# Fused sliding-window attention and MoE on one core: first loads in float32, batch 1 transposed on chip, chunk 0's second matmul in halves

## The chip, the cores and the metric

One core of one Trainium2 chip runs the whole program. The metric is the device time of one execution in microseconds (us), the median of a few runs. In these kernels TensorE does the matmuls, VectorE and ScalarE the elementwise work (in the kernel before 2352, 430 and 288 instructions), GpSimd issues the loads that cast float32 to bfloat16, and SyncE issues the stores and the DMA transposes.

The kernel before varies a good deal from run to run and from chip to chip: 343.7 to 351.1 us within a single set of runs. Times in us are therefore compared only within one set, on one chip; across sets the ratio to the kernel before is compared, which was run beside every set. Runs more than 1.5% above the fastest of their kernel are called slow and left out; this took away 5 of the 11 runs of the kernel before in the second set, 2 of 11 in the third and none in the first, although runs of 350 us occur in all three. So a difference between sets of less than about 0.01 shows little.

## The reference

```python
# q, k, v: float32 [batch 8, heads 8, seq 576, head_dim 64]
# scores = q k^T / 8 + ALiBi bias, causal window of 128, softmax, times v
scores = scale * np.matmul(q, k.transpose(0, 1, 3, 2))
mask = (rel >= 0) & (rel < 128)
scores = np.where(mask, scores + bias[None], -1e9)
attn = np.exp(scores - scores.max(-1, keepdims=True))
attn_out = np.matmul(attn / (attn.sum(-1, keepdims=True) + 1e-9), v)

# tokens of all batches in a row: 4608 x 512, then two matmuls with a gate
x = attn_out.transpose(0, 2, 1, 3).reshape(8 * 576, 512)
h = x @ w_in            # 512 x 2048
g = h * np.cos(h)
out = g @ w_out         # 2048 x 512, float32
```

## The kernel before

The operations are written in program order with their tile dependences; a list scheduler in the kernel assigns each a start with cost constants (`occ`, `lat`), and that fixes, before anything runs, the order of every engine's instructions. Each engine's program holds its list in that order, and in the traces an instruction whose data is late holds those behind it: in the kernel before, TensorE did nothing for the 9.9 us ahead of batch 1's scores, and GpSimd issued no load for 27.7 us while one waited.

Attention of a batch has nine units: eight of two heads and 256 tokens (`G` is 0 or 1), and a tail of 64 tokens. The MoE runs in nine chunks of 512 tokens: `moe1` (64 matmuls of 128x512 outputs and the gate) and `moe2` (64 more). Chunk c is interleaved with the attention of batch c+1. Chunk 2 is tokens 1024 to 1535 and batch 2 begins at token 1152, so chunk 2 needs the first outputs of batch 2's attention soon after they are made.

The loads and the places of q and k:

```python
        def load_piece(w, src, g):
            op("pool", [lambda e: e.dma_start(
                nat[w][0][:, 2 * g:2 * g + 2, :].rearrange("p a (h c) -> p (a h) c", h=4),
                src[0, :, 256 * g:256 * g + 256, :].rearrange("h (s j) d -> s h (j d)", j=2))],
               w=[("nat", w, 0, g)], dma=f"ld{w}0{g}", occ=720, lat=1500)

        def load_nat(w, src, b, t):
            rows = 128 if t < 4 else 64
            op("pool", [lambda e: e.dma_start(
                nat[w][b % 2][0:rows, t, :].rearrange("p (h d) -> p h d", h=H),
                src[b, :, 128 * t:128 * t + rows, :].rearrange("h p d -> p h d"))],
               w=[("nat", w, b % 2, t)] + ([("nat", w, 0, t // 2)] if b % 2 == 0 and t < 4 else []),
               dma=f"ld{w}{b % 2}n{t}", occ=900, lat=7 * rows)
```

For batches 1 to 7 q and k are transposed by DMA, block by block (ten DMA transposes a batch); batch 0 is transposed on TensorE:

```python
        def cross_transposes(b, blocks=range(NBLK)):
            i = b % 2
            for t in blocks:
                rows = 128 if t < 4 else 64
                for w in "qk":
                    op("sp", [lambda e, t=t, rows=rows, w=w: e.dma_start_transpose(
                        tr[w][i][:, :, 128 * t:128 * t + rows], nat[w][i][0:rows, t, :])],
                       r=[("nat", w, i, t)], w=[("tr", w, i, t, hf) for hf in range(2)],
                       dma=f"x{w}{i}{t}", occ=1000, lat=700 if t < 4 else 400, pri=3)
```

The attention output is transposed back either by DMA or on TensorE:

```python
        def x_back(b, u, s, i):
            if u[0] == "t":
                t0 = S * b + 512
                op("sp", [lambda e: e.dma_start_transpose(xT[:, :, t0:t0 + 64], xtl[i][:, :])],
                   r=[("xtl", i)], w=[k_ for pr in range(NPAIR) for k_ in xkeys(pr, t0, 64)],
                   dma=f"xt{i}", occ=700, lat=400, pri=2)
                return
            pr, G = u
            t0 = S * b + 256 * G
            if b >= 4 or (b > 0 and G == 0):
                op("sp", [lambda e: e.dma_start_transpose(
                    xT[:, pr, t0:t0 + 256].rearrange("p (r t) -> p r t", r=2), xnat[i][:, :])],
                   r=[("xnat", i)], w=xkeys(pr, t0, 256), dma=f"xb{i}", occ=700, lat=500, pri=2)
                return
            bank = SLOT[s][0]
            dst = ps[:, bank, :].bitcast(BF16)[:, 768:1024]

            def f(e):
                ins = None
                for r in range(2):
                    ins = e.transpose(dst[:, 128 * r:128 * r + 128],
                                      xnat[i][:, 128 * r:128 * r + 128], ident[:, :])
                return ins
            op("pe", f, r=[("xnat", i), "ident"], w=[("B", bank)], occ=120, lat=290, pri=0)
            flex(xT[:, pr, t0:t0 + 256], dst, [("B", bank)] + xkeys(pr, t0, 256), 256, 0)
```

The second matmul of a chunk, and the order of everything:

```python
        def moe2(c):
            gi = c % 2
            for t in range(4):
                tg = 4 * c + t
                bank = OB[tg % 2]
                oi = tg % NOB
                for fc in range(NFC):
                    op("pe", lambda e, t=t, fc=fc, bank=bank: e.matmul(
                        ps[:, bank, :], gT[gi][:, fc, 128 * t:128 * t + 128], w_out[:, fc, :],
                        start=(fc == 0), stop=(fc == NFC - 1)),
                       r=[("g", gi, fc, t // 2), ("wo", fc // 4)], w=[("B", bank)], occ=216, lat=379,
                       pri=6)
                row = CH * c + 128 * t
                halves = 2 if tg == 4 * NCH - 1 else 1
                wd = 512 // halves
                for hf in range(halves):
                    cs = slice(wd * hf, wd * hf + wd)
                    flex(ob[oi][:, cs], ps[:, bank, cs], [("B", bank), ("ob", oi, hf)], wd, 6)
            # ... [store of the tile]
```

```python
        load_piece("q", q, 0)
        load_piece("k", k, 0)
        constants()
        fills()
        load_v(0, (0, 1))
        masks()
        load_piece("q", q, 1)
        load_piece("k", k, 1)
        load_w_in(0)
        load_nat("q", q, 0, 4)
        load_nat("k", k, 0, 4)
        load_v(0, (2, 3, 4))
        for i, w in enumerate("qk"):
            first_transposes(w, 0, (4, 6)[i])
        for u in range(1, 4):
            load_w_in(u)
        load_w_out(0)
        load_w_out(1)
        for t in range(NBLK):
            load_nat("q", q, 1, t)
            load_nat("k", k, 1, t)
        load_w_out(2)
        load_w_out(3)
        load_v(1)
        us0 = units(0)

        def run(b, us, ns, n0):
            two = [(u, (n0 + j) % ns) for j, u in enumerate(us)]
            scores(b, two)
            for u, s in two:
                exps(b, u, s)
            for u, s in two:
                mask(b, u)
                pv(b, u, s)
                i = norm(b, u, s)
                x_back(b, u, s, i)
        run(0, us0[0:2], 4, 0)
        run(0, us0[2:4], 4, 2)
        for i, w in enumerate("qk"):
            first_transposes(w, 1, (3, 5)[i])
        first_tail(7)
        run(0, us0[4:6], 4, 0)
        run(0, us0[6:8], 4, 2)
        run(0, us0[8:9], 4, 0)
        order = [4, 5, 6, 7, 0, 1, 2, 3]
        for c in range(NCH):
            if c == 0:
                for i in range(NFC):
                    moe1_half(c, i // 8, i % 8, order[i % 8])
            else:
                for fc in range(NFC):
                    moe1(c, fc, 2 + fc % 6)
            if c + 1 < B:
                cross_transposes(c + 1)
                attention(c + 1)
            if c + 2 < B:
                for t in range(NBLK):
                    load_nat("q", q, c + 2, t)
                    load_nat("k", k, c + 2, t)
                load_v(c + 2)
            moe2(c)
```

The softmax here doesn't subtract the row's maximum and nothing guards it: scores larger than these inputs give would overflow.

## Time and profile before

| | before |
|---|---|
| median time | 344.8 us (3 runs, 344.6 to 346.2) |
| span of the profiled execution | 343.6 us |
| TensorE busy | 307.8 us |
| TensorE idle in 36 to 62 us | 9.9 us, mean granted clock 0.80 |
| TensorE idle in 105 to 120 us | 7.3 us, mean granted clock 0.66 |

Four lines of the page of the kernel before: the busy time of each engine; the busy tenths of TensorE and its granted clock in 40 slices of 8.6 us; and the shares of the chain of waits by engine.

```profile
PE 307.8 (90%) x2352; PEld 155.8 (45%) x2352; DVE 191.5 (56%) x430; ACT 203.7 (59%) x288; POOL 105.0 (31%) x133
...
PE   2689809989992899999998999899999999999996
...
PEclk9969967999997699999999999999999999999999
...
PE 77%; DMA 14%; POOL 5%; DVE 1%; ACT 1%; SPq 1%; issue 1%; POOLq 0%; DVEq 0%; ACTq 0%
```

The two dips in the TensorE row, at slices 6 and 13, are the two stalls; the clock row is below 9 beside them. The rest of the row is nearly full, so the kernel can only gain in those places, at the start, or by doing less on TensorE.

Four stretches of the kernel before, with busy time and number of instructions for each engine, then the granted clock, the DMA share and GB/s.

```profile
core 0: us, PE busy (x) PEld busy (x) DVE busy (x) ACT busy (x) POOL busy (x), PEclk, DMA share, GB/s
36.00:62.00 26.00, 16.14 (x120) 9.09 (x118) 7.54 (x19) 8.29 (x12) 0.00 (x0) 0.80 1.83 147
95.00:105.00 10.00, 9.45 (x101) 4.55 (x99) 4.59 (x13) 6.08 (x9) 0.00 (x0) 1.00 1.75 156
105.00:120.00 15.00, 7.68 (x53) 3.99 (x54) 4.04 (x10) 3.04 (x5) 3.64 (x5) 0.66 1.43 131
250.00:282.00 32.00, 31.95 (x260) 15.34 (x257) 22.61 (x51) 22.12 (x30) 0.00 (x0) 1.00 0.19 53
```

The last line is a batch in the steady part: 31.95 of 32.0 us busy. The lines of 36 and 105 us are the stalls.

TensorE's timeline of the kernel before, the instructions with a long idle time ahead of them (start, duration, instruction; in brackets the idle time and what ended it). The count at the end of a line depends on where the listing was cut.

```profile
51.32 1.15 PE L463 MATMUL ps<-qt,kt 64*128 64x256 bf16 x12 [9.87 <-DMA kt<-knat]
...
110.44 0.61 PE L674 MATMUL ps<-xT,w_inb 128*128 128x512 bf16 x1 [5.95 <-DMA xT<-xnat]
112.11 0.61 PE L674 MATMUL ps<-xT,w_inb 128*128 128x512 bf16 x1 [1.06 <-DMA xT<-xnat]
```

The first is batch 1's scores waiting for keys transposed by DMA. The other two are `moe1` of chunk 2 waiting for outputs of batch 2.

SyncE's queue of the kernel before: start and time taken by each issue.

```profile
44.21 3.21 SPq L425 DMA_TRANSPOSE kt<-knat  x1
...
99.50 1.26 SPq L425 DMA_TRANSPOSE qt<-qnat  x1
100.80 1.28 SPq L425 DMA_TRANSPOSE kt<-knat  x1
...
102.75 4.38 SPq L618 DMA_TRANSPOSE xT<-xnat  x3
```

Batch 3's transposes `qt` and `kt` (to 102 us) stand in the list ahead of batch 2's outputs `xT`, and each issue there takes about 1.3 us, for 128x256 (the last line is three of them, 4.38 us together) as for 128x512 elements. From issue to landing the transposes of k took 2.4 to 12.9 us in this run. GpSimd's queue of the kernel before:

```profile
34.05 0.89 POOL L310 DMA_DIRECT2D knat<-in_k_dram  x1
62.62 0.88 POOL L310 DMA_DIRECT2D qnat<-in_q_dram  x1 [27.67 <-DMA knat<-in_k_dram]
```

After the first load of k for batch 2 it waits 27.7 us. In the kernel the key `("nat", w, 0, t // 2)` makes block 1 of an even batch depend on block 0's landing.

The chain of waits of the kernel before in order of time (start, length, piece), as marks of progress: the block of `moe1` of chunk 1, the start of `moe2` of chunk 1, and `moe1` of chunk 2 with 53 matmuls left.

```profile
73.86 13.12 PE ps L674 x60
86.98 1.73 PE ps L704 x8
...
119.77 11.61 PE ps L674 x53
```

### The profile page before, as it was taken

To read this page: it belongs to the slowest core of one execution; us is meant where nothing else is said; L and a number is where in the kernel's file an instruction comes from. 1 tells how busy PE (TensorE), PEld (TensorE's weight loads), DVE (VectorE), ACT (ScalarE), POOL (GpSimd) and SP (SyncE) were. 2 spreads that over 40 slices of the span, in tenths; PEclk is the share of its full clock that TensorE was granted. 3 is DMA by queue.
4 is the path that set the end of the run, shared out by engine and by line. 5 is a ranking of instruction groups with operands and counts; after the bars stand their busy time and mean duration, and the time that the engine had idled before them with its cause. 6 is when DMAs were issued, how large, how long until landed. Compare 5 with 4: busy or idle time off the path is not lost.

```text
span 343.6 us, 6134 instructions
## 1 busy us (share of the span) xinstructions
PE 307.8 (90%) x2352; PEld 155.8 (45%) x2352; DVE 191.5 (56%) x430; ACT 203.7 (59%) x288; POOL 105.0 (31%) x133
## 2 busy tenths in 40 slices
PE   2689809989992899999998999899999999999996
PEld 1468604544450444454454444445544454444442
DVE  3558602568651385658656855784686768365000
ACT  5859703578543287459648865785688378465121
POOL 8997000379900489142434801300000000000000
PEclk9969967999997699999999999999999999999999
DMA  9999999999999999999997999972310220000212
GB/s 80 165 199 188 164 143 125 179 142 146 154 156 158 110 163 165 178 167 154 106 136 116 155 158 121 111 124 55 92 25 31 84 66 15 0 33 32 90 63 93
DMA packets 167405, 39.87 MB, mean 116 GB/s; under 512 B 158544, under 2 KB 162896, under 8 KB 167376
## 3 DMA queue, kind: packets, MB, share of 16 engines
q0 software_dynamic: 112576, 18.36, 80.2%
q1 hardware_dynamic: 54800, 21.12, 33.4%
q8 instruction: 19, 0.31, 0.4%
q14 instruction: 10, 0.08, 0.1%
HBM read 36.70 MB, written 9.44 MB: 134 GB/s over the span
## 4 chain that ended last, share of the span: by engine, by line
PE 77%; DMA 14%; POOL 5%; DVE 1%; ACT 1%; SPq 1%; issue 1%; POOLq 0%; DVEq 0%; ACTq 0%
PE ps L704 35%; PE ps L674 31%; DMA knat<-in_k_dram 5%; DMA xT<-xnat 5%; PE ps L463 4%; DMA kt<-knat 4%; PE ps L556 3%; PE ps L559 1%; POOL vp L319 1%; ACT p L499 1%; POOL w_inb L326 1%; SPq L425 1%; PE ps L542 1%; POOL qnat L303 1%; DVE p L517 1%
## 5 line engine op out<-in xcount | busy, mean ns | idle before, releaser
L704 PE MATMUL ps<-w_outb,gT 128*128 128x512 bf16 x576 | 140.9, 385 | 0.0
L674 PE MATMUL ps<-xT,w_inb 128*128 128x512 bf16 x512 | 116.8, 381 | 10.7 <-DMA xT<-xnat 10.1
L666 DVE TENSOR_TENSOR gT<-ps,cos 128x512 bf16<-128x512 f32 x144 | 94.3, 686 | 27.9 <-ACT cos L660 18.1
L660 ACT ACTIVATE cos<-ps,halfpi 128x512 f32<-128x512 f32 x144 | 94.2, 688 | 22.0 <-PE ps L674 14.0
L674 PEld LDWEIGHTS ps<-xT,w_inb 128*128 128x128 bf16 x512 | 48.5, 98 | 69.1 <-DMA xT<-xnat 12.2
L704 PEld LDWEIGHTS ps<-w_outb,gT 128*128 128x128 bf16 x576 | 52.6, 99 | 55.8 <-issue 3.7
L499 ACT ACTIVATE p<-ps 128x768 bf16<-128x768 f32 (+1 forms) x64 | 54.3, 917 | 34.9 <-PE ps L463 23.8
L310 POOL DMA_DIRECT2D qnat<-in_q_dram x36 | 32.6, 906 | 65.6 <-DMA qnat<-in_q_dram 35.9
L296 ACT ACTIVATE ob<-ps 128x512 f32<-128x512 f32 (+1 forms) x26 | 15.1, 581 | 55.5 <-PE ps L704 55.5
L319 POOL DMA_DIRECT2D vp<-in_v_dram x40 | 34.2, 918 | 44.1 <-PE ps L559 37.2
L310 POOL DMA_DIRECT2D knat<-in_k_dram x36 | 32.8, 912 | 4.9 <-DMA knat<-in_k_dram 4.8
L517 DVE TENSOR_TENSOR p<-p,emask 128x1024 bf16<-128x1024 bf16 x32 | 21.8, 686 | 16.2 <-ACT p L499 16.0
L598 DVE TENSOR_TENSOR xnat<-ps,rec 128x256 bf16<-128x256 f32 x64 | 26.9, 422 | 2.0
L463 PE MATMUL ps<-qt,kt 64*128 64x128 bf16 (+1 forms) x320 | 18.4, 255 | 10.7 <-DMA kt<-knat 9.9
L556 PEld LDWEIGHTS ps<-vp,p 128*128 128x128 bf16 x256 | 18.2, 102 | 18.4 <-issue 13.6
L522 DVE TENSOR_TENSOR p<-p,emask 128x256 bf16<-128x256 bf16 x32 | 9.0, 282 | 30.5 <-ACT p L499 30.1
L556 PE MATMUL ps<-vp,p 128*128 128x65 bf16 x256 | 23.2, 200 | 1.2 <-DVE p L517 0.9
L463 PEld LDWEIGHTS ps<-qt,kt 64*128 64x128 bf16 x320 | 12.9, 99 | 21.0 <-issue 19.0
L559 PE MATMUL ps<-vp,p 128*128 128x65 bf16 x192 | 21.3, 200 | 0.0
L596 DVE RECIPROCAL rec<-ps 128x4 f32<-128x4 f32 x64 | 11.2, 177 | 17.7 <-PE ps L559 17.4
L296 ACT ACTIVATE xT<-ps 128x256 bf16<-128x256 bf16 x15 | 5.7, 384 | 20.7 <-PE ps L628 20.3
L297 DVE COPY ob<-ps 128x512 f32<-128x512 f32 x11 | 7.6, 692 | 18.5 <-PE ps L704 18.5
(52 smaller groups left out, 167.0 us busy)
## 6 DMA issues: line engine op xcount, KB each, us to landing
out_dram<-ob SPq DMA_DIRECT2D x35, 256.0 KB, 2.6
vp<-in_v_dram POOLq DMA_DIRECT2D x32, 128.0 KB, 6.3
qnat<-in_q_dram POOLq DMA_DIRECT2D x28, 128.0 KB, 8.2
knat<-in_k_dram POOLq DMA_DIRECT2D x28, 128.0 KB, 9.1
w_inb<-in_moe_w_in_dram POOLq DMA_DIRECT2D x4, 512.0 KB, 10.4
w_outb<-in_moe_w_out_dram POOLq DMA_DIRECT2D x4, 512.0 KB, 19.7
xT<-xnat SPq DMA_TRANSPOSE x44, 3.2
qt<-qnat SPq DMA_TRANSPOSE x35, 6.5
```

The costliest lines, as they stand in the source:

```text
L310: op("pool", [lambda e: e.dma_start(nat[w][b % 2][0:rows, t, :].rearrange("p (h d) -> p h d", h=H), src[b, :, 128 * t:128 * t + rows, :].r ...
L319: op("pool", [lambda e, t=t, rows=rows: e.dma_start(vp[b % 2][0:rows, t, :, 0:64], v[b, :, 128 * t:128 * t + rows, :].rearrange("h p d -> ...
L463: ins = e.matmul(ps[:, banks[x], c0:c1], keys_ap(i, x, pr, kc), query_ap(i, x, pr, qb, 128 * nb), start=True, stop=True)
L499: op("act", lambda e: e.activation(P[i][:, :, lo:512], src_[:, :, lo:512], ACTF.Exp, scale=0.125), w=held + [("P", i)], occ=920 if u[1] el ...
L517: op("dve", lambda e: e.tensor_tensor(p, p, m, ALU.mult), r=[("P", i), ("EM", 2 * pr), ("EM", 2 * pr + 1)], w=[("P", i)], occ=605, lat=lat ...
L556: ins = e.matmul(o, P[i][:, x, d0:d0 + 128], V[:, kc, h, 0:65], start=True, stop=not two)
L559: ins = e.matmul(o, P[i][:, x, p0:p0 + 128], V[:, kc - 1, h, 0:65], start=False, stop=True)
L598: op("dve", lambda e: e.tensor_tensor(o, U[:, :, :, 0:64], rv[:, :, :, None].broadcast_to([128, 2, 2, 64]), ALU.mult), r=[("rec", ri)], w= ...
L660: op("act", lambda e: e.activation(cosb[ci][:, :], h, ACTF.Sin, bias=halfpi[:, 0:1]), r=["halfpi"], w=[("B", bank), ("cos", ci)], occ=586, ...
L666: op("dve", lambda e: e.tensor_tensor(o, h, cs, ALU.mult), r=[("cos", ci)], w=[("B", bank)] + keys, occ=606, lat=692, pri=3)
L674: op("pe", lambda e, kc=kc: e.matmul(ps[:, bank, :], w_in[:, kc, 128 * fc:128 * fc + 128], xT[:, kc, CH * c:CH * c + CH], start=(kc == 0), ...
L704: op("pe", lambda e, t=t, fc=fc, bank=bank: e.matmul(ps[:, bank, :], gT[gi][:, fc, 128 * t:128 * t + 128], w_out[:, fc, :], start=(fc == 0 ...
```

## The change

The change loads the first 256 tokens of q and k in float32 from SyncE's queue and casts them on VectorE or ScalarE; loads batch 1 in the pair layout (rows of 256 bytes in the buffer in place of 128) and transposes it on TensorE; does `moe2` of chunk 0 in two halves, so that the first half needs only half of `w_out`; loads v of batch 1 before the rest of `w_out`; transposes two blocks at once by DMA for batches 2 to 7; drops the shared keys; and gives the scheduler other costs for SyncE's queue. The name given to the change also says that sums of P times V are kept in score banks; that was so already, only the order of the banks is new.

```diff
-        free = {e: 0 for e in ENG}
+        free = {"pe": 1000, "act": 800, "dve": 1000, "pool": 1300, "sp": 1000}
...
-        tr = {w: [sb(f"{w}t{i}", [128, NPAIR, 640]) for i in range(2)] for w in "qk"}
+        tr = {w: [sb(f"{w}t{i}", [128, NBLK, NPAIR, 128]) for i in range(2)] for w in "qk"}
...
+        def load_first(w, src, hf, i):
+            op("sp", [lambda e: e.dma_start(
+                ob[i][:, :].rearrange("p (h c) -> p h c", h=4),
+                src[0, 4 * hf:4 * hf + 4, 0:256, :].rearrange("h (s j) d -> s h (j d)", j=2))],
+               ...)
+            o, x = nat[w][0][:, hf, :], ob[i][:, :]
+            op(("act", "dve"), {... activation Copy, or tensor_copy ...})
...
-               w=[("nat", w, b % 2, t)] + ([("nat", w, 0, t // 2)] if b % 2 == 0 and t < 4 else []),
+               w=[("nat", w, b % 2, t)],
...
-        def cross_transposes(b, blocks=range(NBLK)):
+        def cross_transposes(b):
             i = b % 2
-            for t in blocks:
-                rows = 128 if t < 4 else 64
+            for t0, t1 in ((0, 2), (2, 4), (4, 5)):
                 for w in "qk":
...
-                       dma=f"x{w}{i}{t}", occ=1000, lat=700 if t < 4 else 400, pri=3)
+                       dma=f"x{w}{i}{t0}", occ=1250, lat=1200 if t0 < 4 else 500, pri=3)
...
-                   dma=f"xt{i}", occ=700, lat=400, pri=2)
+                   dma=f"xt{i}", occ=1250, lat=400, pri=2)
...
         def moe2(c):
+            if c == 0:
+                for u in range(2):
+                    for t in range(4):
+                        moe2_mm(c, t, range(8 * u, 8 * u + 8), t)
+                    if u == 0:
+                        yield
+                for t in range(4):
+                    store(c, t, t)
+                return
...
-        for t in range(NBLK):
-            load_nat("q", q, 1, t)
-            load_nat("k", k, 1, t)
+        for g in range(2):
+            load_piece("q", q, 1, g)
+            load_piece("k", k, 1, g)
+        load_nat("q", q, 1, 4)
+        load_nat("k", k, 1, 4)
+        load_v(1)
         load_w_out(2)
         load_w_out(3)
-        load_v(1)
...
             if c + 1 < B:
-                cross_transposes(c + 1)
-                attention(c + 1)
+                us = units(c + 1)
+                if c == 0:
+                    for g in range(2):
+                        first_transposes("q", 1, g, (4 + 2 * g, 4 + 2 * g))
+                        first_transposes("k", 1, g, (5 + 2 * g, 5 + 2 * g))
+                    for g in range(0, 8, 2):
+                        run(1, us[g:g + 2], (2, 3))
+                    first_tail(1, 6)
+                    run(1, us[8:9], (2,))
+                else:
+                    cross_transposes(c + 1)
+                    for g in range(0, 9, 3):
+                        run(c + 1, us[g:g + 3], (1, 2, 3))
```

## The prediction

> **What bounds it now.** The page: span 343.6 us, TensorE busy 307.8; the chain of waits is 77% TensorE, 14% DMA. From 120 us on it is TensorE-bound: in 250 to 282 us, one batch, TensorE is busy 31.95 of 32.0 us. The loss lies early. TensorE's timeline: idle to 5.75 us, then about 5 us of gaps by 21 us, granted clock 0.50 in 20 to 25 us; 41.4 to 51.3 us, idle 9.9 us for batch 1's key transposes by DMA, then half clock to 55 us, some 2.2 us more; 105 to 120 us, idle 7.5 us for batch 2's transposed outputs, then half clock, some 2.8 us. [...] Later gaps add 2.5 us.
>
> **Why those gaps.** Each DMA transpose takes SyncE's queue 1.25 us to issue[...] (DMA queue's timeline); a batch has ten for q and k. From 82 to 107 us that queue issues without pause: batch 3's transposes stand ahead of batch 2's outputs. GpSimd's queue waits 27.7 us before batch 2's second load, as two blocks share one dependence key.
>
> **What the change does.**
> - First 256 tokens: four float32 loads on SyncE's queue, cast on chip in 0.3 to 0.6 us each. First scores at about 8 instead of 9.0 us; second pieces issue 2 us sooner. Gain 1.5 to 2.5 us.
> - Batch 1's q and k are loaded with rows twice as long and transposed on TensorE: adds 64 transposes, 3.4 us at 53 ns, and evictions of 0.6 to 0.7 us that hide on ScalarE and VectorE. Removes the 9.9 us wait and its cold stretch.
> - moe2 of chunk 0 in halves: 32 matmuls (6.9 us at 216 ns) need only half of w_out and fill the wait for batch 1. But v of batch 1 and the rest of w_out land at an estimated 45 to 50 us, so 3 to 4 us of waits remain. Net gain of this stage 6 to 8 us: chunk 1's moe1 starts near 64 instead of 73.9 us, the start included.
> - Six transposes per batch instead of ten: SyncE saves 5 us a batch. The false dependence is gone, so loads run ahead. The 105 to 120 us stall (10 to 11 us with the cold clock) falls to 1 to 4 us; gain about 8 us.
> - MoE arithmetic is unchanged. PV sums already share the score banks: nothing from that. Later batches stay at 32 us.
>
> Sum: 2 + 7 + 8 + 1.5 (later gaps), 18.5 to 20 us, nearly all on the chain, since TensorE was idle there.
>
> **Predicted: 325 us, 8 in 10 within 316 to 336.** Faster by over 2%: 0.90; within 2%: 0.08; slower: 0.02.
>
> **Right if:** no DMA-transpose wait of batch 1 in the chain; TensorE idle in 36 to 62 us under 5 us; chunk 1's moe1 starts at 60 to 67 us; idle in the stage of batch 2's outputs under 4 us; issue still 1.25 us for two-block transposes; span from chunk 1's start unchanged but for the lost stall.
>
> **Wrong if:** two-block transposes issue in twice the time (the stall near 100 us stays); loads run so deep in GpSimd's queue that v of batch 1, w_out or batch 2's output transposes land late; SyncE, in order, sits behind batch 3's late loads; the schedule, computed ahead with optimistic loads, puts TensorE on data not yet landed; the float32 loads contend with v, so the start gains nothing.

The 5 us a batch in the second stage takes the issue time as the same for two blocks, which was an estimate. The sum is 2 + 7 + 8 + 1.5 = 18.5 us. Some measured times beside those it uses: in the kernel before, the issues of k's transposes took 1.2 to 3.2 us, 1.28 in the median; batch 0's transposes on TensorE took 51 to 80 ns each (8 in 0.41 to 0.64 us), so 53 ns is an estimate; a copy of 128x512 out of a bank took 0.60 us on ScalarE and 0.69 on VectorE; 60 matmuls of 128x512 in a row took 13.12 us, 216 ns apart. Between 82 and 107 us SyncE's queue had one pause of 1.2 us, at 88 us. In the changed kernel a cast of 128x512 took 0.43 us on VectorE and 0.63 us on ScalarE.

## The result and the profile after

The changed kernel took 328.55 us (median of 4, 327.5 to 328.8) against 345.5 us for the kernel before beside it (4 runs). The ratio is 0.9511, interval 0.9472 to 0.9551. A ratio here is the mean time of one kernel's fast runs over that of the other's of the same rounds, so it is not quite the ratio of the medians. The prediction was 325 us, 316 to 336.

The page after, the lines that answer to those shown of before:

```profile
PE 306.8 (94%) x2424; PEld 154.7 (47%) x2424; DVE 195.6 (60%) x439; ACT 205.6 (63%) x293; POOL 99.7 (30%) x127
...
PE   2789899889978999999989999999999999999996
...
PEclk9999999999997999999999999999999999999999
...
PE 80%; DMA 10%; POOL 5%; ACT 2%; DVE 1%; issue 1%; POOLq 0%; ACTq 0%
```

TensorE is busy for as long as before (306.8 against 307.8 us); the dip at slice 6 is gone, and the one near 105 us is now a smaller one in slices 12 and 13. The stretches after, in the columns given above:

```profile
36.00:62.00 26.00, 25.58 (x248) 13.04 (x246) 15.61 (x37) 15.66 (x23) 13.22 (x16) 1.00 1.94 170
95.00:105.00 10.00, 7.42 (x57) 4.02 (x57) 4.48 (x11) 4.14 (x6) 5.03 (x6) 0.83 1.75 184
105.00:120.00 15.00, 15.00 (x80) 6.81 (x79) 10.57 (x17) 13.12 (x20) 6.65 (x9) 1.00 1.89 165
250.00:282.00 32.00, 31.95 (x246) 15.24 (x244) 21.96 (x48) 20.18 (x28) 0.00 (x0) 1.00 0.16 44
```

In 36 to 62 us TensorE is idle 0.4 us instead of 9.9, at full clock. In 95 to 105 us, where the stall of batch 2's outputs now lies, it is idle 2.6 us and the mean clock is 0.83. The steady batch is as it was. TensorE's timeline after, the waits that are left in those places:

```profile
34.00 0.64 PE L402 MATMUL ps<-ident,knat 128*64 128x128 bf16 x16 [1.42 <-DMA knat<-in_k_dram]
...
96.22 0.39 PE L681 MATMUL ps<-xT,w_inb 128*128 128x512 bf16 x1 [1.17 <-DMA xT<-xnat]
97.19 0.39 PE L681 MATMUL ps<-xT,w_inb 128*128 128x512 bf16 x1 [0.58 <-DMA xT<-xnat]
```

A wait for batch 1's keys remains, 1.4 us, now for the load itself. SyncE's queue after:

```profile
73.22 1.24 SPq L440 DMA_TRANSPOSE qt<-qnat  x1
74.96 3.03 SPq L440 DMA_TRANSPOSE kt<-knat  x1
78.09 2.71 SPq L440 DMA_TRANSPOSE qt<-qnat  x1
80.89 3.10 SPq L440 DMA_TRANSPOSE kt<-knat  x1
...
94.95 1.33 SPq L440 DMA_TRANSPOSE qt<-qnat  x1
96.32 1.27 SPq L635 DMA_TRANSPOSE xT<-xnat  x1
```

These `qt` and `kt` transposes carry two blocks each; all but the first of the row take 2.7 to 3.1 us, about twice what one block took. At 94.95 us there is one of batch 4 ahead of batch 2's last output at 96.32 us. The chain after, with the transposes of batch 1 in its first line and then the marks of before:

```profile
36.92 1.08 PE ps L402 x32
...
67.01 10.53 PE ps L681 x48
77.54 1.73 PE ps L707 x8
...
104.03 11.61 PE ps L681 x53
```

The 32 transposes in the first line take 1.08 us, 34 ns each at full clock. By the start of `moe2` of chunk 1 the changed kernel is 86.98 - 77.54 = 9.4 us ahead; at `moe1` of chunk 2 with 53 matmuls left it is 119.77 - 104.03 = 15.7 us ahead; at the end 343.6 - 326.8 = 16.8 us. So 9.4 us came by the end of `moe1` of chunk 1, 6.3 us in the stage of batch 2's outputs, and 1.1 us later. Just before the block of `moe1` of chunk 1 the lead looks smaller (73.86 against 67.01 us), but by then 12 more of its matmuls were done.

The clock, after, in half-microsecond stretches (columns as above):

```profile
95.50:96.00 0.50, 0.00 (x0) 0.00 (x0) 0.34 (x1) 0.50 (x2) 0.00 (x0) 1.00 1.97 155
...
98.50:99.00 0.50, 0.50 (x6) 0.28 (x5) 0.50 (x2) 0.00 (x0) 0.00 (x0) 0.50 2.43 155
```

From 98.3 to 101.7 us it was halved, although the longest gap ahead of it was 1.17 us. In 95 to 98 us TensorE was busy for 1.25 us, so the clock was halved after 3 us that were idle for 1.75 us, and the half clock lasted 3.4 us. In the same profile the clock stayed at 1.00 after the gap of 1.42 us at 34 us, so the length of a gap alone does not decide it. In the kernel before it was halved from 18.3 to 25.1 us with no gap over 1.7 us since 6 us. In the second set's profile of the changed kernel none of the 496 recorded 128x512 matmuls of `moe1` took over 0.39 us, where here they took up to 0.62 us, so that half clock did not come there; but the mean clock in 36 to 62 us was 0.95, here 1.00.

### The profile page after: what moved, and what is told of

Read it like the earlier page. It is cut to its first block, busy times and chain, and to the rows that moved or that the text cites. A ratio compares the mean times of both kernels' runs of the same rounds, so it can differ in the third digit from the quotient of the medians.

```text
span 326.8 us, 6239 instructions
## 1 busy us (share of the span) xinstructions
PE 306.8 (94%) x2424; PEld 154.7 (47%) x2424; DVE 195.6 (60%) x439; ACT 205.6 (63%) x293; POOL 99.7 (30%) x127
## 4 chain that ended last, share of the span: by engine, by line
PE 80%; DMA 10%; POOL 5%; ACT 2%; DVE 1%; issue 1%; POOLq 0%; ACTq 0%
PE ps L707 37%; PE ps L681 32%; DMA knat<-in_k_dram 6%; PE ps L480 4%; DMA xT<-xnat 4%; PE ps L573 3%; POOL vp L332 1%; PE ps L576 1%; ACT p L516 1%; POOL w_inb L339 1%; POOL qnat L303 1%; PE ps L559 1%; PE ps L696 1%; PE ps L402 1%; PE ps L470 0%
## 5 line engine op out<-in xcount | busy, mean ns | idle before, releaser
L707 PEld LDWEIGHTS ps<-w_outb,gT 128*128 128x128 bf16 x576 | 51.9, 98 | 53.9 <-issue 1.3
L323 POOL DMA_DIRECT2D qnat<-in_q_dram x32 | 28.3, 886 | 13.8 <-PE ps L424 9.2
L323 POOL DMA_DIRECT2D knat<-in_k_dram x32 | 28.4, 887 | 6.6 <-issue 5.9
L573 PEld LDWEIGHTS ps<-vp,p 128*128 128x128 bf16 x256 | 17.5, 99 | 19.9 <-issue 13.7
L573 PE MATMUL ps<-vp,p 128*128 128x65 bf16 x256 | 22.7, 197 | 0.9 <-DVE p L534 0.5
L576 PE MATMUL ps<-vp,p 128*128 128x65 bf16 x192 | 20.7, 196 | 0.0
L480 PE MATMUL ps<-qt,kt 64*128 64x128 bf16 (+1 forms) x320 | 17.5, 244 | 0.1
L480 PEld LDWEIGHTS ps<-qt,kt 64*128 64x128 bf16 x320 | 12.1, 95 | 10.6 <-issue 8.5
L696 PE MATMUL ps<-xT,w_inb 128*128 128x256 bf16 x128 | 15.5, 273 | 0.0
L576 PEld LDWEIGHTS ps<-vp,p 128*128 128x128 bf16 x192 | 14.4, 99 | 0.5 <-issue 0.3
## 6 DMA issues: line engine op xcount, KB each, us to landing
w_outb<-in_moe_w_out_dram POOLq DMA_DIRECT2D x4, 512.0 KB, 18.5
```

The costliest lines, as they stand in the source:

```text
L323: op("pool", [lambda e: e.dma_start(nat[w][b % 2][0:rows, t, :].rearrange("p (h d) -> p h d", h=H), src[b, :, 128 * t:128 * t + rows, :].r ...
L480: ins = e.matmul(ps[:, banks[x], c0:c1], keys_ap(i, x, pr, kc), query_ap(i, x, pr, qb, nb), start=True, stop=True)
L573: ins = e.matmul(o, P[i][:, x, d0:d0 + 128], V[:, kc, h, 0:65], start=True, stop=not two)
L576: ins = e.matmul(o, P[i][:, x, p0:p0 + 128], V[:, kc - 1, h, 0:65], start=False, stop=True)
L707: op("pe", lambda e, fc=fc: e.matmul(ps[:, bank, :], gT[gi][:, fc, 128 * t:128 * t + 128], w_out[:, fc, :], start=(fc == 0), stop=(fc == N ...
```

## The experiments

Each undoes or adds one thing and runs in five rounds beside the kernel before. My theory was that of the prediction: the gain of the first stage comes from batch 1's transposes on TensorE, with the halves of `moe2` as filling, and the gain of the second stage from fewer DMA transposes and from the dropped keys. The rivals are that the gain comes from order, that the loads set the pace anyway, or that one part did all of it. All twelve runs gave a correct result. The medians and ranges below are of all six executions; one of them was slow in the runs with the old costs, with the first tokens by GpSimd and with the keys alone, and two in the run with the shared keys. The ratios leave these out.

### First set (kernel before 349.0 us on this chip)

The changed kernel itself was not in this set. Its ratio was 0.951 in each of the three sets that have it (0.9511, 0.9508, 0.9510), and that is what these four are held against; on this chip 0.951 would be 331.9 us. But here no run of the kernel before was left out as slow. With every run counted on both sides the changed kernel's ratio is 0.947, 0.946 and 0.949 in its three sets, and these four have 0.941, 0.964, 0.952 and 0.939.

**Ten DMA transposes instead of six.** Only SyncE's list changes.

```diff
-            for t0, t1 in ((0, 2), (2, 4), (4, 5)):
+            for t0, t1 in ((0, 1), (1, 2), (2, 3), (3, 4), (4, 5)):
-   ... lat=1200 if t0 < 4 else 500
+   ... lat=700 if t0 < 4 else 400
```

> The changed kernel (328.5 us) with q and k of batches 2 to 7 again transposed block by block, ten DMA transposes a batch instead of six; TensorE, VectorE, ScalarE and GpSimd keep their order. Theory (SyncE's issue time set the stall before moe1 of chunk 2): four more issues of 1.25 us make SyncE about 5 us later in each batch, the gap of 2.6 us and its half clock near 95 to 105 us grow to 6 us or more: 331 to 335 us. Rival (the stall shrank for another reason, the order of SyncE's queue or the loads): within 1 us of 328.5.

Measured: 328.5 us (326.1 to 329.9), ratio 0.9401 (0.9353 to 0.9449). SyncE's queue in this run, for the same stretch as above:

```profile
77.50 1.36 SPq L440 DMA_TRANSPOSE kt<-knat  x1
78.90 1.30 SPq L440 DMA_TRANSPOSE qt<-qnat  x1
80.25 1.29 SPq L440 DMA_TRANSPOSE kt<-knat  x1
```

One block takes 1.3 us, so two take what one two-block transpose takes in the changed kernel. For all of batch 3 the ten issues take 13.6 us of the queue and the six 12.6, where the prediction had 5 us less. TensorE's gaps at `moe1` of chunk 2 are 0.9 and 0.8 us, against 1.2 and 0.6 in the changed kernel; in 95 to 105 us it is idle 2.1 us at a clock of 1.00, against 2.6 us at 0.83. Ten are not slower than six. The theory falls for this part: SyncE saved next to nothing here, and the stall shrank for another reason. Whether ten are truly faster is not shown, as the measure was not on the same chip.

**The shared keys put back.** GpSimd's list is unchanged, only its waits come back; SyncE's order is computed anew.

```diff
-               w=[("nat", w, b % 2, t)],
+               w=[("nat", w, b % 2, t)] + ([("nat", w, 0, t // 2)] if b % 2 == 0 and t < 4 else []),
```

> The changed kernel with the shared dependence keys of the kernel before put back for the loads of q and k of even batches; every engine but SyncE keeps its order. Theory: GpSimd's queue waits for landings again (some 20 us before batch 2's second load), batch 2's and 3's loads come later, their transposes stand in SyncE's queue and the stall near 100 us grows: 331 to 336 us. Rival (loads were early enough anyway): within 1 us of 328.5, with the waits of GpSimd's queue back but nobody waiting for it.

Measured: 335.2 us (333.7 to 340.8), ratio 0.9583 (0.9533 to 0.9633), which is 0.007 or about 2.5 us above the changed kernel's (the intervals overlap); the profiled spans differ by 5.2 us (332.0 and 326.8, on two chips). GpSimd's queue in this run, and TensorE's wait for batch 2's outputs:

```profile
48.26 0.88 POOL L323 DMA_DIRECT2D qnat<-in_q_dram  x1 [21.25 <-ACT p L516]
```

```profile
102.35 1.03 PE L681 MATMUL ps<-xT,w_inb 128*128 128x512 bf16 x2 [6.97 <-DMA xT<-xnat]
```

GpSimd waits 21.3 us again ahead of batch 2's second load, and the stall near 100 us is one gap of 7.0 us, as in the kernel before. (The name in the bracket of the first line is only the last event seen before the wait ended.) So in the changed kernel the dropped keys are worth 2.5 to 5 us (4.0 us if the fast runs are set against all runs of the kernel before). The size rests on different chips; that the wait and the stall come back with the keys is in the trace.

**The old costs in the scheduler.** SyncE's `occ` back to 1000, 700 and 60, `lat` of stores to 600, and the first starts to 0.

> The changed kernel, but its schedule computed with the old costs of SyncE's queue (transposes 1.0 and 0.7 us, stores 0.06 us, all engines starting at 0) instead of 1.25 and 0.4 us. Nothing else changes but order. Theory (the saved issues and loads did it, the costs are a detail): within 2 us of 328.5. Rival (the truer costs set a better order of SyncE's queue and that is where the gain near 100 us came from): 332 to 337 us with the stall near 100 us back at 8 us or more.

Measured: 332.0 us (329.5 to 336.3), ratio 0.9485 (0.9433 to 0.9537). Not distinguishable from 0.951. The profile has a new wait of 3.0 us at 105.6 us, with a mean clock of 0.89 in 105 to 120 us, and is idle 3.5 us in 95 to 105 us against 2.6; the 8 us stall of the rival did not come. So the costs did not make the large gains. That they are worth nothing is not shown: 332.0 us is some 3 us above the changed kernel on its three other chips (328.6 to 329.5 us).

**Batch 2's first outputs transposed on TensorE.**

```diff
-            if b >= 4 or (b > 0 and G == 0):
+            if b >= 4 or (b in (1, 3) and G == 0):
```

> The changed kernel with batch 2's first four attention outputs transposed on TensorE (8 transposes and 4 evictions more) instead of by DMA. Theory (the remaining stall of 2.6 us and its half clock near 95 to 105 us is only the wait for these DMA transposes): both go, TensorE adds about 1 us, so 325 to 326.5 us. Rival (something behind it, the tail of attention or batch 3's data, sets the pace there): within 1 us of 328.5.

Measured: 327.2 us (326.5 to 329.2), ratio 0.9384 (0.9342 to 0.9426), lower than 0.951 by 0.0126 or 4.4 us. The two waits for `xT` near 96 us and the half clock are gone. What is left of the stall is the wait for those DMA transposes and nothing behind it. By these ratios the gain is larger than the 2 to 3.5 us expected; with every run of the kernel before counted it is 2.9 us (0.939 against 0.947), as expected. The measure is from other chips; the last set below checks it.

### Second set (kernel before 347.6 us)

**The changed kernel again.**

> The changed kernel unaltered, as the measure for the three runs beside it on this chip (the kernel before was 345.5 us on one chip and 349.0 us on another, so runs of different calls cannot be compared in us). Every theory: 0.951 of the kernel before within its interval (0.947 to 0.955), near 0.947 if the first call's ten-transpose run at 0.940 was only slightly faster.

Measured: 328.8 us (328.1 to 330.1), ratio 0.9508 (0.9464 to 0.9551). Span 328.3 us.

**The first 256 tokens by GpSimd's queue again.**

```diff
-        for i, (w, src, hf) in enumerate((("q", q, 0), ("k", k, 0), ("q", q, 1), ("k", k, 1))):
-            load_first(w, src, hf, i)
+        load_piece("q", q, 0, 0)
+        load_piece("k", k, 0, 0)
```

> The changed kernel with the first 256 tokens loaded and cast by GpSimd's queue again. Theory (the start is worth 1.5 to 2.5 us on the chain): 2 to 3 us longer than the changed kernel. Rival (what the start gains is spent again in the wait for batch 1's k near 34 to 37 us, because the loads and not TensorE set that time): within 1 us of the changed kernel, and that wait shorter or gone.

Measured: 332.2 us (329.7 to 335.8), ratio 0.9595 (0.9533 to 0.9657): 3.4 us longer by the medians, though the intervals of the ratios overlap. Both kernels ran side by side, so their fast runs can be set against each other: 329.7 to 333.5 us (5 runs, mean 331.6) and 328.1 to 330.1 us (6 runs, mean 329.1), 2.6 us longer with a 95% interval of 0.7 to 4.4. That agrees with the theory. The profiled executions do not show it: span 328.0 against 328.3 us, the block of `moe1` of chunk 1 with 47 matmuls left at 69.20 against 68.99 us. There the wait for batch 1's keys is 2.0 us at 36.2 us against 1.8 us at 34.5 us, so the loads came 1.8 us later and the time was made up by 69 us. But the profile here is of this kernel's fastest run, and that of the changed kernel of its slowest of the set. In the changed kernel's two other profiles the block starts at 67.0 and 67.1 us with 48 left, some 2 us ahead of this one. So the start is worth about 2.6 us by the timed runs; the trace of this set does not show where.

**Batch 1 by DMA transposes again**, its loads in blocks of 128 tokens; the halves of `moe2` kept.

```diff
-        for g in range(2):
-            load_piece("q", q, 1, g)
-            load_piece("k", k, 1, g)
-        ...
+        for t in range(NBLK):
+            load_nat("q", q, 1, t)
+            load_nat("k", k, 1, t)
 ...
-                    for g in range(2):
-                        first_transposes("q", 1, g, ...)
-                        first_transposes("k", 1, g, ...)
+                    cross_transposes(1)
```

> The changed kernel with batch 1's q and k loaded in blocks of 128 tokens and transposed by DMA again, the halves of moe2 kept. Theory (transposes on TensorE took away the 10 us wait and its cold stretch): TensorE idle again for some 5 to 10 us between 36 and 60 us, less than before because half of moe2 fills it; 4 to 8 us longer than the changed kernel. Rival (the halves of moe2 alone cover the wait, and the transposes cost TensorE as much as they save): within 1.5 us.

Measured: 342.2 us (341.6 to 345.3), ratio 0.9904 (0.9849 to 0.9960), 13.4 us longer than the changed kernel beside it. TensorE's waits in this run, first the stage of batch 1, then that of batch 2's outputs:

```profile
45.11 0.82 PE L480 MATMUL ps<-qt,kt 64*128 64x256 bf16 x8 [7.60 <-DMA kt<-knat]
...
57.89 1.03 PE L707 MATMUL ps<-w_outb,gT 128*128 128x512 bf16 x2 [3.52 <-DMA w_outb<-in_moe_w_out_dram]
```

```profile
112.38 1.35 PE L681 MATMUL ps<-xT,w_inb 128*128 128x512 bf16 x2 [7.06 <-DMA xT<-xnat]
```

The wait for batch 1's keys is back (7.6 us). The half of `moe2` did not fill it: in TensorE's list five of its matmuls stand ahead of batch 1's first scores (at 36.3 us) and the others behind them. A new wait of 3.5 us for the second half of `w_out` follows; its slowest load landed 32.9 us after its issue. And the stall of batch 2's outputs is back too, 7.1 us. In the profiles, 8.5 us of the loss is there at `moe1` of chunk 1 (77.27 us with 48 matmuls left against 68.99 with 47) and the rest of 341.7 - 328.3 = 13.4 us, 4.9 us, comes after it. So this one part carries most of the gain of both stages. It is larger than either theory had it. What drives the second stage here is, by the traces, that everything issued behind these transposes is later; the last set has a run that parts them from their loads.

**`moe2` of chunk 0 whole.**

```diff
-            if c == 0:
-                for u in range(2):
-                    ...
-                return
```

> The changed kernel with moe2 of chunk 0 done whole, tile by tile in two banks, after attention of batch 1 in the program. Theory (half of moe2 fills the wait for batch 1's data and for w_out's second half): 2 to 5 us longer than the changed kernel, with TensorE waiting for w_out or for batch 1's exponentials between 40 and 60 us. Rival (the transposes on TensorE suffice): within 1 us.

Measured: 330.4 us (328.8 to 331.2), ratio 0.9538 (0.9491 to 0.9585), 1.6 us longer by the medians and 1.0 us by the means (interval -0.1 to 2.2). TensorE is idle 0.6 us in 36 to 62 us in both profiles of this set. The theory's 2 to 5 us did not come: the halves are worth about 1 us or nothing. With batch 1 on TensorE there is nothing long to fill.

### Third set (kernel before 346.9 us)

**The changed kernel, third time.**

> The changed kernel unaltered, the measure for the three runs beside it on this chip. Every theory: 0.951 of the kernel before, as in the two calls that have it.

Measured: 329.5 us (328.5 to 332.1), ratio 0.9510 (0.9466 to 0.9555).

**The kernel before with the keys alone dropped.** The lists of TensorE, VectorE, ScalarE and GpSimd are unchanged.

```diff
-               w=[("nat", w, b % 2, t)] + ([("nat", w, 0, t // 2)] if b % 2 == 0 and t < 4 else []),
+               w=[("nat", w, b % 2, t)],
... [the loads of 256 tokens and their transposes name both blocks' keys]
```

> The kernel before with one thing done: its loads of q and k no longer share dependence keys; TensorE, VectorE, ScalarE and GpSimd keep their order. Theory (the shared keys held GpSimd's queue and so made batch 2's and 3's data and the stall at 105 to 120 us late): the 27.7 us wait of GpSimd's queue goes and the stall shrinks by 4 to 8 us, 0.977 to 0.988 of the kernel before. Rival (SyncE's queue, which issues without pause from 82 to 107 us, holds that stall): within 1%.

Measured: 348.8 us (344.7 to 350.7), ratio 1.0014 (0.9952 to 1.0077). TensorE's waits in this run:

```profile
51.47 1.14 PE L463 MATMUL ps<-qt,kt 64*128 64x256 bf16 x12 [12.19 <-DMA kt<-knat]
...
77.68 7.64 PE L674 MATMUL ps<-xT,w_inb 128*128 128x512 bf16 x28 [2.35 <-DMA xT<-xnat]
...
112.03 0.61 PE L674 MATMUL ps<-xT,w_inb 128*128 128x512 bf16 x1 [1.95 <-DMA xT<-xnat]
...
119.35 1.90 PE L674 MATMUL ps<-xT,w_inb 128*128 128x512 bf16 x8 [1.40 <-DMA xT<-xnat]
```

GpSimd's 27.7 us wait is gone, and the gap ahead of `moe1` of chunk 2 fell from 6.0 and 1.1 us to 2.0 us. From the start of `moe2` of chunk 1 to the last 53 matmuls of chunk 2 it now takes 119.35 - 91.58 = 27.8 us instead of 119.77 - 86.98 = 32.8 us: 5.0 us gained. But `moe2` of chunk 1 starts 4.6 us later. Batch 1's keys are not the reason. Their wait is longer (12.2 us instead of 9.9) only because TensorE came to it 2.2 us sooner; the scores start at 51.47 us, against 51.32. The loss comes after it: `moe1` of chunk 1 now waits 2.4 us for the last of batch 1's outputs and then runs slower: 28 matmuls take 7.64 us, 1.4 us more than at 216 ns each, which would be half clock until about 80.6 us (an estimate from that). SyncE's queue shows what it waits for:

```profile
68.05 1.33 SPq L425 DMA_TRANSPOSE qt<-qnat  x1
...
70.06 1.19 SPq L618 DMA_TRANSPOSE xT<-xnat  x1
```

With batch 2's data earlier in the schedule, three of batch 2's transposes stand ahead of this output in SyncE's new list. It is issued at 70.06 us, where the kernel before had issued it by 66.2, and lands 7.6 us later, where batch 1's outputs in the kernel before took 2.9 to 5.1 us. So the gain was given back: the wait moved from batch 2's outputs to batch 1's, by SyncE's order and by slower landings, which no run parts. In the changed kernel batch 1's outputs of that kind are issued from 45.2 us, before any of batch 2's transposes; that fits with the keys paying there, but is argued from the traces.

**Batch 1 with short rows, still on TensorE.** Loads by block as in the run with DMA transposes, 32 full 128x128 transposes in place of 64 half ones.

```diff
+        def block_transposes(w, b, g, bank):
+            for i in range(2):
+                t = 2 * g + i
+                ...
+                        ins = e.transpose(dst[:, 128 * pr:128 * pr + 128],
+                                          nat[w][b][:, t, 128 * pr:128 * pr + 128], ident[:, :])
 ...
-                        first_transposes("q", 1, g, (4 + 2 * g, 4 + 2 * g))
-                        first_transposes("k", 1, g, (5 + 2 * g, 5 + 2 * g))
+                        block_transposes("q", 1, g, 4 + 2 * g)
+                        block_transposes("k", 1, g, 5 + 2 * g)
```

> The changed kernel with batch 1's q and k loaded block by block (rows of 128 bytes in the buffer instead of 256) but still transposed on TensorE, as 32 full transposes. It parts the two halves of the batch 1 change, which the run with DMA transposes (13 us longer than the changed kernel) undid together. Theory (the transposes by DMA cost the time, in their own wait and in holding up the loads behind them): 0 to 3 us longer than the changed kernel. Rival (the longer rows did it, by getting v, w_out and batch 2 in sooner): 6 us longer or more, w_out's second half landing near 57 us as there.

Measured: 329.6 us (329.0 to 330.3), ratio 0.9502 (0.9464 to 0.9540), equal to the changed kernel. The longer rows are worth nothing that can be seen. The slowest load of `w_out` landed 20.5 us after its issue, against 32.9 us in the run with the DMA transposes, whose loads and load order are the same. So it was the DMA transposes that held up the loads behind them.

**What the runs point to.** Ten DMA transposes a batch, and the first outputs of batches 2 and 4 on TensorE.

```diff
-            if b >= 4 or (b > 0 and G == 0):
+            if b >= 5 or (b == 4 and G == 1) or (b in (1, 3) and G == 0):
```

> The changed kernel with what the first runs point to: ten DMA transposes a batch, and the first four outputs of batches 2 and 4 transposed on TensorE. Theory (ten cost nothing, 0.940 against 0.951; the stalls near 100 and 168 us are the wait for those outputs, 4 us and 1.3 us, less 1 us each of TensorE's time): 0.935 to 0.943 of the kernel before, about 3 us less than the changed kernel. Rival (the differences between the first calls are the chips'): within 1 us of the changed kernel beside it.

Measured: 326.3 us (325.8 to 328.0), ratio 0.9419 (0.9380 to 0.9458), 3.2 us less than the changed kernel beside it. The stretch of the stall in the changed kernel of this set, then in this one:

```profile
95.00:105.00 10.00, 7.13 (x55) 3.80 (x55) 4.62 (x11) 3.70 (x5) 3.87 (x5) 0.83 1.78 177
```

```profile
95.00:105.00 10.00, 9.10 (x96) 4.49 (x94) 5.36 (x13) 6.92 (x10) 4.28 (x6) 1.00 1.90 185
```

TensorE busy rises from 7.13 to 9.10 of 10 us and the clock from 0.83 to 1.00. This version beats both kernels. As it has both edits and gains 3.2 us, the 3.4 us by which ten transposes alone seemed faster in the first set was at least partly an effect of comparing across sets.

## Why the prediction was right, and where it was wrong

The total was 3.5 us too hopeful, inside the range. That it came so near is in part luck: the gain of the second stage was put down to fewer issues and to the dropped keys, and the first of these gave nothing. By terms:

| term | predicted | profile |
|---|---|---|
| start and stage of batch 1 | 2 + 7 = 9 us | 9.4 us |
| stage of batch 2's outputs | 8 us | 6.3 us |
| later gaps | 1.5 us | 1.1 us |
| sum | 18.5 us | 16.8 us |

- **Batch 1's transposes** ("Removes the 9.9 us wait and its cold stretch"): right, and shown by undoing it (13.4 us). The cost was overestimated: 64 transposes at 34 ns make 2.2 us, not 3.4. The residual waits were too: idle in 36 to 62 us is 0.4 us, with 1.4 us more at 34 us, not 3 to 4. The estimate that v and `w_out` would make TensorE wait did not come true.
- **The halves of moe2** ("fill the wait for batch 1"): not shown. Without them the time is 1.0 us longer by the means, with an interval of -0.1 to 2.2.
- **The step that failed** is "Six transposes per batch instead of ten: SyncE saves 5 us a batch". The issue time per instruction was read from transposes of 128x256 and 128x512 in the kernel before and carried over to 128x1024. The trace of the kernel before already held the warning: the issue at 44.21 us took 3.2 us for one block (and the one ahead of it 4.5 us), so the time is not fixed. In the loaded stretch those took 2.7 to 3.1 us, so 1.0 us was saved for batch 3 and not 5, and ten instead of six cost nothing (0.9401). The prediction named this case under what would make it wrong, and half of that came true: the issue time doubled, yet the stall shrank.
- **"The false dependence is gone, so loads run ahead"**: right in part. In the changed kernel the keys are worth 2.5 to 5 us. In the kernel before they are worth nothing: the 5.0 us gained in the stage of batch 2's outputs are lost in the stage before, where batch 1's last output now stands behind batch 2's transposes. The prediction had the two as separate terms of a sum; the runs show that the second pays only once the first is done.
- **The mis-sized term** is the second stage, 8 predicted and 6.3 measured. The stall fell from 7.3 us idle in a stretch with a mean clock of 0.66 to 2.6 us idle in one of 0.83, where I had allowed 1 to 4 us in all; the half clock that stayed (3.4 us at 0.50, by estimate 1.7 us lost) is what I left out. What remains is the DMA transposes of batch 2's outputs, standing in SyncE's list behind other transposes and landing 6.5 to 7.7 us after their issue; moved to TensorE they gain 3 us.
- **The start**: second scores of batch 0 at 16.28 instead of 18.05 us, 1.8 us, as predicted, and no half clock at 20 to 25 us. By the timed runs 2.6 us of it reach the end (interval 0.7 to 4.4).
- The marks set out: no DMA-transpose wait of batch 1, right; idle under 5 us in 36 to 62, right; `moe1` of chunk 1 at 60 to 67, its block is at 67.0 and its first matmul at 57.5; idle under 4 us in the stage of batch 2, right (2.6 us); issue of 1.25 us for two blocks, wrong under load, right later (1.26 us at 134 us); the rest unchanged, right.

Open: why the two-block transposes take twice as long in one stretch and not in another. The DMA share is 1.93 in 74 to 84 us, where they took 2.7 to 3.1 us, and 0.67 in 134 to 137 us, where they took 1.26; whether the load is the cause is not shown, no run varied it. Also open is where the start's gain lies after 36 us, and why the half clock near 98 us comes in some executions of the changed kernel (the mean clock in 95 to 105 us was 0.83 in two profiles) and not in the second set's.

## What to carry to other kernels

When two stalls lie one behind the other and wait for the same queue, their causes do not add up: dropping the keys gave nothing while batch 1 was transposed by DMA, since the gain of one stage was lost in the stage before, and 2.5 to 5 us once it was transposed on TensorE. So undo parts of a change from the finished kernel and also add them one by one to the old one. A per-instruction cost read at one size need not be the cost at twice the size (here 1.3 us for one block, 2.7 to 3.1 us for two in the loaded stretch and 1.26 us later): measure the new shape under the same load before counting what fewer instructions save. Where an engine's order is fixed ahead, look for what stands in front of the late item in its list, and move the item to an engine with time to spare, as the last version did (TensorE had been idle 2.9 of 10 us there).
